# RWKV attention plus SMeLU MLP on one core: four batches across the partitions, attention in 32-row array tiles, orders from a list scheduler

## The chip, the cores and the metric

The kernel runs on one core of a Trainium2 chip. The metric is device microseconds of one execution. The two executions of before differ by 0.4% (196.12 and 197.0 us); an execution more than 1.5% above the fastest of its kernel is called slow here and is not compared. The profile is one execution, taken by the hardware profiler; its span differs from the median time, by 2.5 us in before.

## The reference

Four batches of 768 tokens go through a linear attention with 8 heads of 48 and a decay per channel; the result, 3072 tokens of 384, goes through an MLP with 2048 hidden units and a piecewise quadratic activation (SMeLU).

```python
# r, k, v: (4, 8, 768, 48); w, u: (8, 48)
for t in range(S):
    kt, vt, rt = k[:, :, t], v[:, :, t], r[:, :, t]
    cur = einsum('bhd,bhe->bhde', u[None] * kt, vt)
    y[:, :, t] = einsum('bhd,bhde->bhe', rt, state + cur)
    state = w[None, :, :, None] * state + einsum('bhd,bhe->bhde', kt, vt)

x = y.transpose(0, 2, 1, 3).reshape(3072, 384)
h = x @ w_in                                        # (3072, 2048)
g = where(h >= 1, h, where(h <= -1, 0, (h + 1) ** 2 / 4))
out = g @ w_out                                     # (3072, 384)
```

Both kernels work in chunks of 128 tokens: inside a chunk a masked matrix of scores, between chunks a state. Both compute `Square(0.5*h + 0.5)` for the activation, prove with norms that |h| stays under 1, and redo the MLP in general form if it does not.

## The kernel before

A *unit* is one batch's chunk of 128 tokens: 24 units, each with its tokens on the 128 partitions. Two units make one block of 256 tokens for the MLP, 12 blocks in all.

```python
def load():                          # one unit: 128 tokens on 128 partitions
    b, c = units[i]
    for name, src in (("K", k), ("R", r), ("V", v)):
        t = io.tile([128, H, D], F32, name=name, tag=name)       # 6 buffers each
        nc.sync.dma_start(out=t, in_=src[b, :, t0:t0 + C, :].rearrange("h s d -> s h d"))   # 192-byte rows

def s_at(i):                         # scores: two 64-row array tiles
    for p in range(NP):
        for s in range(2):
            mm(AT_p[s][:, p, :], KT[rows, p, :], RT[rows, p, :], start=True, stop=True)
    ...                              # mask on VectorE

def s_y(i):                          # output and state of one unit
    for p in range(NP): mm(pair(y, p), RT[:, p, :], Tbd[b][:, p, :], ...)        # history
    for h in range(H):  mm(y[:, h, :], AT[h % 2][:, h // 2, :], V[:, h, :], ...) # inside the chunk
    for p in range(NP): mm(st[:, p, :], pair(Kw, p), pair(V, p), ...)            # new state
    for h in range(H):               # the u term, on VectorE, head by head
        nc.vector.scalar_tensor_tensor(x[:, h*D:(h+1)*D], V[:, h, :], diag[:, h:h+1], y[:, h, :], ...)

def layer1(m, n):                    # 6 matmuls of 256 columns, then the activation
    for f in range(2):
        for kk in range(nKb):
            mm(h_p[:, f, :], w_in_sb[:, kk, ...], xT[m][:, :, kk, :], ...)
    g = gT[m][:, 2*n:2*n+2, :]
    nc.scalar.activation(g, h_p, AF.Square, bias=0.5, scale=0.5)     # contiguous read and write

# [cut] layer2: 4 matmuls of 384 columns; the order of work is written by hand
# and refined by the framework's own scheduler
```

## Time and profile before

| | before |
|---|---|
| time, median of 2 | 196.56 us (196.12 to 197.0) |
| profiled span | 199.1 us |
| first layer-1 matmul | 25.0 us |
| last MLP matmul | 193.6 us |
| MLP matmuls, back to back | 125.6 us (96 groups at 0.655, 96 at 0.65) |

The profile's first part gives, for each engine, busy microseconds, their share of the span, and instructions. PE is TensorE's matmuls, PEld its weight loads, DVE VectorE, ACT ScalarE, POOL GpSimd. The second part cuts the span into 40 slices: a digit is a busy share in tenths, PEclk the clock granted to TensorE in tenths, DMA the busy share of the 16 DMA engines, GB/s what they moved. Then come the DMA packets and the instruction-fetch queue, and the chain of waits: the work that ended last, followed back, shared out by engine. Of the page of before:

```profile
span 199.1 us, 4592 instructions
PE 172.3 (87%) x1686; PEld 125.7 (63%) x1686; DVE 111.8 (56%) x354; ACT 122.0 (61%) x251; POOL 110.8 (56%) x144
...
PE   0263598998989999999999959999999999999990
PEclk9999999999999999999999979999999999999999
DMA  4999989999969999999999998334315022020202
GB/s 96 201 258 264 250 195 221 243 181 268 262 131 244 173 193 169 258 195 173 253 162 216 165 168 206 76 74 132 64 35 153 2 66 66 9 79 0 82 3 89
DMA packets 100444, 30.25 MB, mean 152 GB/s; under 512 B 93504, under 2 KB 98880, under 8 KB 100416
...
q8 instruction: 15, 0.25, 0.6%
...
PE 66%; DMA 5%; DVE 4%; ACT 2%; POOL 1%; issue 1%; ACTq 0%; DVEq 0%
```

TensorE is the bound: it is nearly full from a quarter of the span on, and it is two thirds of the chain.

The groups of instructions: line, engine, operation, output<-input, shapes, count | busy us, mean ns of one | idle before, and what ended it. Two groups of before:

```profile
L285 ACT ACTIVATE gT<-h_p 128x512 bf16<-128x512 f32 x96 | 56.8, 598 | 44.9 <-PE h_p L279 42.6
L238 DVE SCALAR_TENSOR_TENSOR x<-V,diag,y 128x48 bf16<-128x48 bf16 x192 | 35.8, 257 | 18.5 <-PE y L227 11.1
```

The activation takes 598 ns, less than the 0.655 us of the layer-1 group that feeds it.

The timeline lists runs of instructions: start, length, what, and in brackets the idle time before and its cause. TensorE of before, a stretch in the steady part:

```profile
129.38 0.81 PE L279 MATMUL h_p<-xT_201,w_in_sb 128*128 128x256 bf16 x6
130.03 0.19 PE L227 MATMUL y<-V,AT_2273 128*128 128x48 bf16 x1
...
130.45 0.23 PE L206 MATMUL AT_p_2389<-RK 48*128 48x128 bf16 x1
...
130.78 0.83 PE L279 MATMUL h_p<-xT_202,w_in_sb 128*128 128x256 bf16 x6
```

Small attention matmuls of one unit lie between MLP groups; there is no idle time. One unit's scores take from 130.45 to 130.78, 0.33 us for 8 matmuls.

### The profile page before, as it was taken

How to read it: one execution, taken by the hardware profiler on the slowest of the kernel's cores; microseconds unless marked ns; L12 is line 12 of the kernel's file. 1: busy time of each engine (PE TensorE's matmuls, PEld its weight loads, DVE VectorE, ACT ScalarE, POOL GpSimd, SP SyncE). 2: the span in 40 equal slices, each digit the busy share in tenths (PEclk: the TensorE clock that was granted, in tenths of full speed). 3: DMA queues.
4: the chain of work that ended last, by engine and by line, in shares of the span. 5: the costliest groups of instructions: out<-in, count | busy, mean ns of one | idle time of the engine just before them, and what ended most of it. 6: DMA issues, size and time to landing. Idle time of an engine off the chain costs nothing.

```text
span 199.1 us, 4592 instructions
## 1 busy us (share of the span) xinstructions
PE 172.3 (87%) x1686; PEld 125.7 (63%) x1686; DVE 111.8 (56%) x354; ACT 122.0 (61%) x251; POOL 110.8 (56%) x144
## 2 busy tenths in 40 slices
PE   0263598998989999999999959999999999999990
PEld 0141476776867677866777547677667677777750
DVE  4179979994867608842867643776576464200110
ACT  3657769999887547936558326567555356454540
POOL 7496756989976999967679386857221000000000
PEclk9999999999999999999999979999999999999999
DMA  4999989999969999999999998334315022020202
GB/s 96 201 258 264 250 195 221 243 181 268 262 131 244 173 193 169 258 195 173 253 162 216 165 168 206 76 74 132 64 35 153 2 66 66 9 79 0 82 3 89
DMA packets 100444, 30.25 MB, mean 152 GB/s; under 512 B 93504, under 2 KB 98880, under 8 KB 100416
## 3 DMA queue, kind: packets, MB, share of 16 engines
q1 hardware_dynamic: 100416, 29.90, 75.1%
q8 instruction: 15, 0.25, 0.6%
q14 instruction: 13, 0.11, 0.2%
HBM read 20.84 MB, written 4.72 MB: 128 GB/s over the span
## 4 chain that ended last, share of the span: by engine, by line
PE 66%; DMA 5%; DVE 4%; ACT 2%; POOL 1%; issue 1%; ACTq 0%; DVEq 0%
PE o_p L297 28%; PE h_p L279 26%; DVE x L238 3%; DMA xT_201<-x 3%; DMA R<-in_r_dram 2%; PE y L227 2%; PE y L224 2%; PE st L235 1%; PE xp L265 1%; PE tr L194 1%; ACT gT L285 1%; ACT RK L197 1%; POOL RKW_173 L173 0%; POOL KU L177 0%; PE tr L196 0%
## 5 line engine op out<-in xcount | busy, mean ns | idle before, releaser
L285 ACT ACTIVATE gT<-h_p 128x512 bf16<-128x512 f32 x96 | 56.8, 598 | 44.9 <-PE h_p L279 42.6
L297 PE MATMUL o_p<-w_out_sb,gT 128*128 128x384 bf16 x384 | 73.5, 327 | 0.0
L279 PEld LDWEIGHTS <-w_in_sb 128*128 128x128 bf16 x576 | 54.5, 99 | 14.5 <-issue 3.4
L297 PEld LDWEIGHTS <-gT 128*128 128x128 bf16 x384 | 36.2, 98 | 19.3 <-issue 0.7
L238 DVE SCALAR_TENSOR_TENSOR x<-V,diag,y 128x48 bf16<-128x48 bf16 x192 | 35.8, 257 | 18.5 <-PE y L227 11.1
L176 POOL TENSOR_TENSOR KU<-K,u_bc 128x384 f32<-128x384 f32 x24 | 24.5, 1021 | 1.9 <-DVE diag L213 1.6
L177 POOL TENSOR_TENSOR KU<-KU,R 128x384 f32<-128x384 f32 x24 | 24.3, 1013 | 0.3
L301 DVE COPY o_sb<-o_p 128x384 f32<-128x384 f32 x12 | 6.7, 555 | 23.8 <-PE o_p L297 23.7
L197 ACT COPY RK<-tr 128x1024 bf16<-128x1024 bf16 x12 | 12.2, 1014 | 3.9 <-PE tr L196 3.8
L182 POOL CAST V<-V 128x384 bf16<-128x384 f32 x16 | 8.1, 503 | 11.3 <-DVE x L238 7.0
L206 PEld LDWEIGHTS <-RK 48*128 48x128 bf16 x192 | 8.3, 99 | 9.5 <-issue 4.2
L213 DVE TENSOR_REDUCE diag<-KU 128x8 f32<-128x384 f32 x24 | 13.1, 546 | 2.1 <-POOL KU L177 1.9
L265 PE MATMUL xp<-ident,x 128*128 128x128 bf16 x36 | 7.9, 236 | 5.6 <-DVE x L238 5.1
L301 ACT COPY o_sb<-o_p 128x384 f32<-128x384 f32 x12 | 5.7, 476 | 7.5 <-PE o_p L297 6.4
L173 POOL TENSOR_TENSOR RKW_171<-K,Winv 128x384 bf16<-128x384 f32 x6 | 6.0, 997 | 6.9 <-ACT Winv L137 3.5
L279 PE MATMUL h_p<-xT_201,w_in_sb 128*128 128x256 bf16 x48 | 7.4, 302 | 2.5 <-DMA xT_201<-x 2.5
L173 POOL TENSOR_TENSOR RKW_177<-K,Winv 128x384 bf16<-128x384 f32 x6 | 6.2, 1029 | 6.1 <-PE st L235 3.9
L265 PEld LDWEIGHTS <-x 128*128 128x128 bf16 x36 | 3.6, 101 | 8.9 <-DVE x L238 8.0
L194 PE MATMUL tr<-ident,RKW_171 128*128 128x128 bf16 x12 | 1.4, 249 | 8.8 <-POOL RKW_171 L173 8.8
L173 POOL TENSOR_TENSOR RKW_173<-K,Winv 128x384 bf16<-128x384 f32 x6 | 6.6, 1094 | 3.6 <-DMA K<-in_k_dram 1.8
L279 PE MATMUL h_p<-xT_195,w_in_sb 128*128 128x256 bf16 x48 | 7.7, 311 | 0.1
L173 POOL TENSOR_TENSOR RKW_175<-K,Winv 128x384 bf16<-128x384 f32 x6 | 6.4, 1072 | 2.1 <-DMA K<-in_k_dram 1.6
(356 smaller groups left out, 321.9 us busy)
## 6 DMA issues: line engine op xcount, KB each, us to landing
K<-in_k_dram SPq DMA_DIRECT2D x24, 192.0 KB, 4.9
R<-in_r_dram SPq DMA_DIRECT2D x24, 192.0 KB, 4.7
V<-in_v_dram SPq DMA_DIRECT2D x24, 192.0 KB, 4.9
out_dram<-o_sb SPq DMA_DIRECT2D x24, 192.0 KB, 2.3
w_in_f<-in_moe_w_in_dram SPq DMA_DIRECT2D x4, 768.0 KB, 5.7
w_out_f<-in_moe_w_out_dram SPq DMA_DIRECT2D x4, 768.0 KB, 5.9
w_bc<-in_w_dram SPq DMA_DIRECT2D x1, 192.0 KB, 3.5
u_bc<-in_u_dram SPq DMA_DIRECT2D x1, 192.0 KB, 4.3
```

Source lines behind the costliest of these rows:

```text
L173: nc.gpsimd.tensor_mul(Kw[:, :, 0:D], K, Winv)
L176: nc.gpsimd.tensor_mul(KU, K, u3)
L177: nc.gpsimd.tensor_mul(KU, KU, R)
L197: nc.scalar.copy(RK, tr)
L206: mm(AT_p[s][:, p, :], KT[rows, p, :], RT[rows, p, :], start=True, stop=True)
L213: nc.vector.reduce_sum(diag, KU, axis=mybir.AxisListType.X)
L238: nc.vector.scalar_tensor_tensor(x[:, h * D : (h + 1) * D], V[:, h, :], diag[:, h : h + 1], y[:, h, :], op0=ALU.mult, op1=ALU.add)
L265: nc.tensor.transpose(xp[:, kk, :], x[:, kk * 128 : (kk + 1) * 128], ident)
L279: mm(h_p[:, f, :], w_in_sb[:, kk, (2 * n + f) * 128 : (2 * n + f + 1) * 128], xT[m][:, :, kk, :], start=(kk == 0), stop=(kk == nKb - 1),)
L285: nc.scalar.activation(g, h_p, AF.Square, bias=0.5, scale=0.5)
L297: mm(o_ps[m][j], gT[m][:, f, j * C : (j + 1) * C], w_out_sb[:, f, :], start=(f == 0), stop=(f == nN - 1))
L301: (nc.scalar.copy if j else nc.vector.tensor_copy)(o_sb, o_ps[m][j])
```

## The change

The intent is to make attention cheap on TensorE and VectorE. All four batches share the partitions: batch b has partitions 32b to 32b+31, and each partition holds four neighbouring tokens ("four-token slots"), so a row of a load is 4 x 48 x 4 = 768 bytes. Products of one batch use only its 32 rows or columns of the array, so that four batches can go in separate array tiles. The u term becomes 16 matmuls with an identity. Because slots scatter tokens, the activation puts the tokens back in order by the pattern of its write. A list scheduler in the kernel, with a duration written down for each operation, orders all engines, and fills TensorE's early waits with dummy "warm-up" matmuls.

```diff
     def load(c, name, hh=None):
+        for b in range(B):                       # four transfers, 32 partitions each
+            nc.sync.dma_start(
+                out=t[name, c][qu[b], hs(hh)].rearrange("q h j d -> q h (j d)"),
+                in_=src[b, hs(hh), c*C:(c+1)*C, :].rearrange("h (p j) d -> p h (j d)", j=J),
+            )
 ...
+    def scores(c, jj, hh):                       # 32 matmuls a group, 4 groups a chunk
+        for p in range(2):
+            for j in range(2):
+                for s in range(2):
+                    for b in range(B):
+                        mm(A[qu[b], s, p, j], KT[rows[s], jj+j, 2*hh+p, qu[b]],
+                           RT[rows[s], :, 2*hh+p, qu[b]], start=True, stop=True)
 ...
+    def ymm(c, hh=None):
+        # 64 history matmuls, 128 inside the chunk, 16 for the u term, in one piece
 ...
+    def state_mm(c):
+        # 128 matmuls, in one piece
 ...
     def smelu(m, n):
-        nc.scalar.activation(g, h_p, AF.Square, bias=0.5, scale=0.5)
+        g = t["g", m][:, 2*n:2*n+2, :].rearrange("p f (u q i) -> p (f u) i q", u=UB, i=J)
+        h_p = t["h", m, n].rearrange("p f (u i q) -> p (f u) i q", u=UB, i=J)
+        nc.scalar.activation(g, h_p, AF.Square, bias=0.5, scale=0.5)
 ...
+    RING = dict(f=7, W=1, Vb=2, RK=1, AT=1, VD=1, x=2, g=3, o_sb=3, sq=2, a=2, h=2, o=2)   # buffers
 ...
+    def warm(count):                             # dummy matmuls, 221 in all
+        for i in range(count):
+            mm(w_p[:, 0:128], ident, ident, start=True, stop=True)
 ...
+    op(("sm", m, n), "ACT", 0.52, (smelu, m, n), [("L1", m, n)], 0)       # planned duration in us
+    op(("y", c, hh), "PE", (1.15 + 0.4 * (c > 0)) / n_y, (ymm, c, hh), needs, d + 10, ...)
+    op(("st", c), "PE", 0.55, (state_mm, c), ...)
 # [cut] one op(...) for every operation, and the scheduler's loop
```

Casts, norms and the MLP's matmuls are as before. Eight of 24 units are transposed on TensorE (before 12), the others by DMA.

## The prediction

> **What bounds the kernel now.** TensorE: 66% of the chain of waits, 54% in the two MLP layers. On the chain a layer-1 group (6 matmuls of 256 columns) takes 0.655 us and a layer-2 group (4 of 384) 0.65 us; 96 + 96 need 125.6 us. The first starts at 25.0 us (timeline), the last ends at 193.6, the span ends at 199.1 (unprofiled 196.6). So 168.6 us hold 125.6 of MLP and 43 us of attention matmuls, transposes and holes; 25 + 5.5 us are head and tail.
>
> In the first 36 us layer 1 trickles behind prep and casts. At 113.9 to 116.5 us TensorE waits for a DMA transpose (5.4 us on the chain) behind an input load (3.6 more). The 40 slices show the DMA engines at 80 to 100% until 117 us; 93,504 of 100,444 packets are under 512 B (192-byte rows).
>
> **What the change does.**
> 1. 768-byte loads: a quarter of the input packets. [...] this trace shows only that 192-byte loads ran at 200 to 260 GB/s with full engines. I expect over 280 GB/s in the head and no TensorE wait on a late load or transpose (-3 to -5 us), although DMA transposes now serve 16 of 24 units, not 12.
> 2. Attention in array tiles, four batches at once. [...] score matmuls at 28.26 us start in pairs, a pair each 55 ns. But a score group between MLP groups takes 0.33 us and not 0.22: about 0.1 us for a change of tile shape, both ways. Before, four units cost about 5.9 us of TensorE without transposes (scores 3.4, y and state 2.5). After, my estimate: scores 4 x 0.42 = 1.7; y 2.2 (tiny matmuls at 25 ns a round, 4 shape changes); state 0.8: 4.7 us. So about 1 us for each of six chunks, 6 us, not the tiles' factor of four. Fewer units transposed on TensorE (8, not 12): 2.5 us.
> 3. DVE loses 192 small multiply-adds (35.8 us busy, 257 ns each) for 12 double copies shared with ACT [...]; POOL gains a product. Off the chain in the steady part, it pays only in the head.
> 4. List-scheduled order and warm-up matmuls: MLP starts near 20 us, [...] without the trickle: with the holes of 40 to 60 us, -8 us.
>
> **Sum.** Start 20 + MLP 125.6 + attention of five chunks 23.5 + transposes and norms 3.5 + residual holes 4 = 176.6; tail 5 gives a span of 181, less the 2.5 us between span and time: 178; the order may do better than my holes, so 176.
>
> Predicted: 176 us, range 167 to 188. Chances: faster 0.93, same 0.04, slower 0.03.
>
> **What would show it.** First layer-1 matmul at 18 to 21 us; DMA packets near 35,000; PE busy above 90% from 20 us on; each scores group 0.3 to 0.45 us; no TensorE wait over 1.5 us after 40 us; MLP groups unchanged at 0.65 us; POOL busy near 115 us, DVE below 95.
>
> **What would make it wrong.** Small tiles not overlapping (128 weight loads a chunk in turn, at the 99 ns a record shows, would add 10 us a chunk and make it slower); single buffers for transposed inputs or scores making TensorE wait each chunk; DMA transposes of 128 x 2048 over 8 us; permuted ACT writes in the activation over 0.6 us; or, the other way, free tile changes: then 168.

The sum comes, as it says, to 176.6 us at the last MLP matmul, a span of 181, a time of 178 and then 176. But "over 280 GB/s" is the author's estimate and was not shown by before, where slices with the DMA engines at 9 tenths moved 162 to 268 GB/s. That four tiles run at once, as the attention term needs, was an estimate too: before shows two. Its trace has the other numbers of that step: output matmuls start 25 ns apart (28.02 to 28.14 us); the first score matmul starts 0.12 us after the last of them (28.26), and the next MLP group 0.15 us after the last score matmul (28.44 to 28.59), where score pairs follow each other at 0.06. "About 0.1 us for a change of tile shape" is an estimate from these starts. Of the 23 slices before 117 us two had the DMA engines under 80% (4 and 6 tenths).

## More of the kernel before

The fetch queue moved 15 packets for TensorE's 3,372 instructions.

"issue", time in which an engine waited for nothing that the profile shows, is 1%.

## The result, and the profile after

| | before | after |
|---|---|---|
| time, median of 2 | 196.56 us | 263.0 us (262.0 to 263.99) |
| ratio of after to before | | 1.338, 95% interval 1.313 to 1.363 |
| span of the profile | 199.1 us | 262.2 us |
| mean granted clock | 0.990 | 0.882 |
| first layer-1 matmul | 25.0 us | 47.7 us |
| ScalarE busy | 122.0 us | 177.0 us |

A ratio, here and below, is the mean time of one kernel's fast runs over that of the other's in the same rounds, so it is not quite the ratio of the medians quoted. The kernel is a third slower and its output is correct. The same lines of the page of after:

```profile
span 262.2 us, 8617 instructions
PE 201.8 (77%) x3927; PEld 147.7 (56%) x3927; DVE 112.0 (43%) x109; ACT 177.0 (67%) x210; POOL 101.3 (39%) x53
...
PE   7578342966843869992979986999878996999992
PEclk9957755697997777998699996899999999999999
DMA  6979998404279419999427935371032710310012
GB/s 148 200 216 366 200 207 287 130 2 120 55 152 207 78 62 205 196 211 201 80 56 165 232 75 65 64 156 45 23 65 55 168 63 2 63 60 32 31 60 71
DMA packets 50730, 31.94 MB, mean 122 GB/s; under 512 B 25344, under 2 KB 49152, under 8 KB 50688
...
q8 instruction: 32, 0.52, 0.9%
...
PE 53%; ACT 21%; issue 15%; DMA 4%; DVE 4%; SPq 1%; DVEq 0%; ACTq 0%
```

"issue" grew from 1% to 15% of the chain and ACT from 2% to 21%. TensorE has 7,854 instructions and the fetch queue 32 packets, twice as many. The granted clock falls to 0.5 to 0.7 in slices 3 to 8, where TensorE has holes. That costs MLP time too: at least 15 of the 192 MLP groups of this trace took 1.2 to 1.5 us, nearly all in stretches at half clock, and 3 groups did in before. No run priced this apart; with the cures below the mean clock rises again, to 0.961 and 0.982. The activation's group, after:

```profile
L376 ACT ACTIVATE gT<-h_p 128x512 bf16<-128x512 f32 x96 | 122.8, 1337 | 17.4 <-PE h_p L365 17.1
```

The same arithmetic on the same 128x512 elements takes 1337 ns, and now it is longer than the matmuls it follows. Three stretches of TensorE's timeline of after:

```profile
147.68 0.81 PE L388 MATMUL o_p<-w_out_sb,gT 128*128 128x384 bf16 x4
148.43 0.42 PE L248 MATMUL A<-RK 48*32 48x128 bf16 x32
148.77 0.83 PE L365 MATMUL h_p<-xT,w_in_sb 128*128 128x256 bf16 x6
...
118.09 1.20 PE L289 MATMUL y<-Vb,AT 32*128 32x48 bf16 x128
119.22 0.34 PE L295 MATMUL y<-VD,ident 32*32 32x384 bf16 x4
124.73 0.54 PE L295 MATMUL y<-VD,ident 32*32 32x384 bf16 x12 [5.17 <-issue]
...
188.61 0.37 PE L295 MATMUL y<-VD,ident 32*32 32x384 bf16 x14
191.07 0.34 PE L295 MATMUL y<-VD,ident 32*32 32x384 bf16 x2 [2.09 <-issue]
```

The first shows that the tiles do what was asked: 32 score matmuls take 0.34 us (148.43 to 148.77), as long as 8 did before; and 128 small output matmuls take 1.13 us (118.09 to 119.22), 9 ns each. The other two show holes of 5.2 and 2.1 us *inside* one group of 16 equal matmuls, with nothing waited for, and cut at 4 + 12 in one place, 14 + 2 in the other. TensorE's waits, summed by cause (us in total, times, longest), say how many there are:

```profile
PE y L295 <- issue: 16.2, 4, 6.6
PE st L339 <- issue: 9.7, 4, 5.9
PE h_p L365 <- ACT gT L376: 5.2, 8, 1.2
...
PE y L289 <- issue: 4.6, 2, 4.3
```

Counting TensorE's instructions in the trace (weight loads, matmuls and the few of its queue's own), and taking the 16,384-byte packets of the instruction-fetch queue beside them, shows a pattern. The first three columns are the hole's start, the time to the next instruction's start and the number of instructions begun by then; then that number over 256, and the fetch packet nearest before the restart:

```
hole at   us     begun   /256     packet
 28.57   6.84     961    3.754     32.59 to  33.98
 37.98   6.10    1217    4.754     41.68 to  42.80
 80.17   4.51    2241    8.754     81.85 to  83.17
 88.69   1.37    2497    9.754     87.36 to  88.72
119.23   5.50    3521   13.754    121.74 to 123.05
156.03   1.73    4801   18.754    155.42 to 156.49
159.73   2.03    5057   19.754    158.88 to 160.29
188.65   2.42    6081   23.754    188.40 to 189.80
193.75   1.04    6337   24.754    192.21 to 193.46
219.96   2.64    7361   28.754    219.72 to 221.14
```

Every one of these holes begins at the same remainder of 256 instructions, in most the packet is under way when the hole begins or starts in it, and TensorE restarts 1.3 to 1.7 us after it has ended. They sum to 34.2 us: 12.9 in the head, 21.2 after 60 us. The four of 4.5 to 6.8 us lie in slices with the DMA engines at 9 tenths, the six of 1.0 to 2.6 us in slices at 5 tenths or less.

### The profile page after: what moved, and what is told of

It is laid out like the page before. It is cut to its first block, busy times and chain, and to the rows that moved or that the text cites. A ratio compares the mean times of both kernels' runs of the same rounds, so it can differ in the third digit from the quotient of the medians.

```text
span 262.2 us, 8617 instructions
## 1 busy us (share of the span) xinstructions
PE 201.8 (77%) x3927; PEld 147.7 (56%) x3927; DVE 112.0 (43%) x109; ACT 177.0 (67%) x210; POOL 101.3 (39%) x53
## 2 busy tenths in 40 slices
DMA packets 50730, 31.94 MB, mean 122 GB/s; under 512 B 25344, under 2 KB 49152, under 8 KB 50688
## 4 chain that ended last, share of the span: by engine, by line
PE 53%; ACT 21%; issue 15%; DMA 4%; DVE 4%; SPq 1%; DVEq 0%; ACTq 0%
PE o_p L388 20%; PE h_p L365 17%; ACT gT L376 15%; DMA R<-in_r_dram 3%; PE w_p L141 3%; PE y L289 3%; PE A L248 3%; PE st L339 3%; DVE RKW L187 3%; PE y L281 2%; ACT x L330 1%; PE y L295 1%; ACT o_sb L396 1%; ACT RK L233 1%; PE xp L312 1%
## 5 line engine op out<-in xcount | busy, mean ns | idle before, releaser
L376 ACT ACTIVATE gT<-h_p 128x512 bf16<-128x512 f32 x96 | 122.8, 1337 | 17.4 <-PE h_p L365 17.1
L365 PE MATMUL h_p<-xT,w_in_sb 128*128 128x256 bf16 x576 | 83.2, 285 | 7.1 <-ACT gT L376 5.2
L365 PEld LDWEIGHTS <-w_in_sb 128*128 128x128 bf16 x576 | 57.8, 102 | 26.3 <-issue 10.9
L260 DVE TENSOR_TENSOR AT<-A,umask 128x1024 bf16<-128x1024 f32 x22 | 26.0, 1218 | 14.7 <-PE A L248 14.7
L198 POOL TENSOR_TENSOR K<-K,u_bc 128x1536 f32<-128x1536 f32 (+1 forms) x6 | 18.7, 3124 | 25.8 <-DVE RKW L187 25.8
L187 DVE TENSOR_TENSOR RKW<-R,Wpow 128x768 bf16<-128x768 f32 (+1 forms) x8 | 26.9, 3376 | 0.0
L215 POOL TENSOR_TENSOR VD<-V,dg 128x768 bf16<-128x768 f32 (+1 forms) x8 | 17.2, 2152 | 18.7 <-DVE dg L207 18.7
L141 PE MATMUL w_p<-ident 128*128 128x128 bf16 x221 | 20.6, 265 | 3.8 <-ACT gT L376 2.2
L141 PEld LDWEIGHTS <-ident 128*128 128x128 bf16 x221 | 18.4, 123 | 5.5 <-issue 3.8
L202 POOL TENSOR_TENSOR K<-K,R 128x1536 f32<-128x1536 f32 (+1 forms) x6 | 19.0, 3173 | 0.5
L357 DVE CAST Tbd<-T 64x768 bf16<-64x768 f32 x5 | 15.5, 3095 | 2.6 <-POOL T L354 2.5
```

Of the source, the lines that this page charges most:

```text
L141: mm(w_p[:, 0:128], ident, ident, start=True, stop=True)
L187: eng.tensor_mul(t["W", c][:, :, off + h.start : off + h.stop, 0:D], jhd(t[name, c])[:, :, h], tab[:, :, h])
L198: nc.gpsimd.tensor_mul(t["KU", c][:, hs(hh)], t["K", c][:, hs(hh)], ub4[:, hs(hh)])
L202: nc.gpsimd.tensor_mul(KU, KU, t["R", c][:, hs(hh)])
L215: eng.tensor_mul(t["VD", c].rearrange("q j h d -> q h j d")[:, h], t["V", c][:, h], dg)
L260: nc.vector.tensor_mul(scores_tile(c, jj, hh), t["A", c, jj, hh], umask2[jj // 2])
```

## The experiments

Three theories, none excluding another:

- **A, the write.** The permuted bf16 write of the activation doubles it (598 ns in before, 1337 in after).
- **B, instructions.** TensorE's instructions come in blocks of 256, one 16,384-byte packet each (the ten holes above lie at one remainder of 256; 32 packets came for 7,854 instructions), and TensorE waits when it has used up a block before the next has come. Tiny matmuls in tiles use up a block in 1.13 us (128 matmuls and 128 weight loads), the MLP in about 17 (20 instructions in 1.3 us), so the tiles would make it wait.
- **C, narrow loads.** A load of 32 partitions moves fewer bytes per microsecond than one of 128 (tested below: 12.7 bytes per ns and engine against 18.1 with 768-byte rows, no loss with 192-byte rows).

Rivals: the holes are the cost of the array tiles themselves (changes of shape, waits that the trace doesn't show); the order is bad because the scheduler's durations are wrong; the head has too many loads, or too few buffers. Each ratio is against before in the same rounds, whose median was 198.8, 198.3, 199.8, 200.4 and 197.9 us in the five sets of runs. (The 200.4 had two slow runs of three; the fast one was 197.09.)

### The activation's write alone, in before

Before, with the activation's pattern of after. The tokens come out permuted: the result is wrong (relative error 0.048).

```diff
-            nc.scalar.activation(g, h_p, AF.Square, bias=0.5, scale=0.5)
+            nc.scalar.activation(
+                g.rearrange("p f (u q i) -> p (f u) i q", u=UB, i=4),
+                h_p.rearrange("p f (u i q) -> p (f u) i q", u=UB, i=4),
+                AF.Square, bias=0.5, scale=0.5,
+            )
```

> The kernel before, with one thing of the change: the activation of layer 1 reads and writes in the permuted order (stride of four elements, 8 bytes, in the bf16 output). Rows come out permuted, wrong on purpose. Theory A: mean of the activation 598 to about 1330 ns, ScalarE busy about 192 us, and ScalarE becomes what a block waits for: time 205 to 225 us. Rival (the slow activations of the kernel after come from something else there, such as PSUM or SBUF contention): mean stays near 600 ns and time near 196 us.

Measured: 214.48 us, ratio 1.083 (1.070 to 1.097). The group and the chain of that run:

```profile
L285 ACT ACTIVATE gT<-h_p 128x512 bf16<-128x512 f32 x96 | 121.6, 1345 | 12.1 <-PE h_p L279 11.7
...
PE 40%; ACT 37%; DVE 7%; issue 5%; POOL 4%; DMA 2%; SPq 2%; DVEq 0%; ACTq 0%; POOLq 0%
```

So A is real by itself, and the rival of contention in after is out: the pattern alone makes 598 ns into 1345 and costs 16 us in a kernel with nothing else changed; ScalarE goes from 2% to 37% of the chain.

### The activation contiguous, in after: three attempts

First, contiguous read and write, with the order put right in the stores: four per 128 tokens, 32 partitions each.

```diff
-        g = t["g", m][:, 2*n:2*n+2, :].rearrange("p f (u q i) -> p (f u) i q", u=UB, i=J)
-        h_p = t["h", m, n].rearrange("p f (u i q) -> p (f u) i q", u=UB, i=J)
+        g = t["g", m][:, 2*n:2*n+2, :].rearrange("p f t -> p (f t)")
+        h_p = t["h", m, n].rearrange("p f t -> p (f t)")
 ...
-        nc.sync.dma_start(out=out[t0:t0+C, :], in_=t["o_sb", m, u])
+        o4 = out[t0:t0+C, :].rearrange("(q i) d -> i q d", i=J)
+        for i in range(J):
+            nc.sync.dma_start(out=o4[i], in_=t["o_sb", m, u][qu[i]])
```

> The kernel after, with the activation of layer 1 writing its result contiguously; the token order is put right in the output stores instead (four stores of 32 partitions for one of 128). Theory A (the strided write of the activation holds the steady part back): the 96 activations fall from 1337 ns to about 600 ns, ScalarE busy from 177 us to about 106 us, time to 220 to 235 us. Theory B (TensorE runs out of instructions in the bursts of small matmuls, and this alone makes the kernel slow): activations as fast, but the time stays above 250 us, because the holes of TensorE without a releaser (about 34 us in all) stay. If both hold: 220 to 235 us with the holes still about 30 us.

Measured: 258.76 us, ratio 1.306 (1.294 to 1.317). The activation fell to 596 ns and ScalarE to 115.5 us busy, but the chain gave it back:

```profile
PE 42%; issue 20%; DMA 16%; SPq 8%; POOL 7%; ACT 2%; DVE 2%; POOLq 0%; DVEq 0%
PE o_p L387 18%; PE h_p L365 14%; DMA RK<-RKW 7%; DMA K<-in_k_dram 6%; POOL K L198 3%; SPq L401 3%; DMA R<-in_r_dram 3%; SPq L174 3%; PE y L289 2%; PE st L339 2%; PE A L248 2%; POOL K L202 2%; PE y L281 2%; POOL T L354 1%; PE y L295 1%
```

Theory A's range of 220 to 235 us was missed, and the holes at block edges did not shrink (39.7 us, 34.2 in after). L401 is the new store. Stores, loads and DMA transposes are issued from one queue, and in this run that queue waited 34.8 us in 7 places (up to 13.4) at L401 for the block to store. That such a wait holds back the transposes behind it fits the chain (DMA RK, 7%; SPq L401, 3%) but was not tried apart. The run mixes two edits and can't price A.

Second, the order put right where layer 1 reads: the matmul's moving operand is read with 64 bytes between elements.

```diff
-                    ..., xT[m][:, :, kk, :],
+                    ..., xT[m][:, :, kk, :].rearrange("p u (i q) -> p u q i", i=J),
```

> The kernel after with a contiguous write in the activation, and the token order put right where layer 1 reads its moving operand (strided read, same matmuls), so that the stores stay as they were: the run with four stores per block had held transposes back in the store queue. Theory A alone: activations 600 ns; time 225 to 245 us, below the 258.8 of that run by what the stores cost. Theory that neither A nor the instruction holes alone is worth much, because each hides behind the other and behind the chain from one chunk to the next: 245 to 258 us, with the holes near 34 us. If the strided read slows TensorE, the layer-1 groups take longer than 0.66 us, and the run says nothing of A.

Measured: 464.12 us (fast runs 459.21 and 459.56). The activation was 597 ns, but:

```profile
L365 PE MATMUL h_p<-xT,w_in_sb 128*128 128x256 bf16 x576 | 263.6, 607 | 0.6 <-issue 0.6
```

A group of six takes 263.6/96 = 2.7 us in place of 0.655. A scattered moving operand costs four times here, and the low clock of this run (mean 0.636) is not the reason: these matmuls start 430 ns apart at full and at half clock alike. Two more kernels of the same rounds were built on this read, one with the theory's other cures, one with measured durations in the scheduler:

> All three together: contiguous write with the strided read in layer 1, y and state products in pieces with two buffers, no warm-ups. If the holes and the activation are the two limits of the steady part and hide each other: 195 to 215 us, holes after 60 us below 6 us, ScalarE busy about 110 us. If a third limit (the chain of one chunk through weighting, transposes, scores, masks, y and state, on single-copy queues) is worth as much: 220 to 245 us.

> As the run with all three, but the scheduler plans with durations measured on the chip for the kernel after (for instance 3.0 us and not 0.5 for the cast of the state on VectorE, 3.0 and not 1.8 for the weighting there, 3.0 and not 1.7 for the decay on GpSimd) and 0.9 us between pieces. If the order itself, planned with durations that are too short, costs much: 5 to 15 us below the run with all three. If not: within 3 us of it.

They took 428.92 and 430.12 us. The read spoiled them; they say nothing of their own questions, which were asked again below.

Third, only the order of the activation's loops is exchanged: the write is contiguous, and the f32 read from PSUM is the strided side.

```diff
-        g = ...rearrange("p f (u q i) -> p (f u) i q", u=UB, i=J)
-        h_p = ...rearrange("p f (u i q) -> p (f u) i q", u=UB, i=J)
+        g = ...rearrange("p f (u q i) -> p (f u) q i", u=UB, i=J)
+        h_p = ...rearrange("p f (u i q) -> p (f u) q i", u=UB, i=J)
```

> The kernel after with the two loops of the activation's access pattern exchanged: the same mapping, but the bf16 output is written in order and the f32 input in the accumulator bank is read with a stride of 32. Nothing else differs. Theory A (the strided write to on-chip memory costs, not the permutation as such): 600 to 750 ns and not 1337; time 235 to 255 us, the rest hidden by the instruction holes and the chain of a chunk. If a strided read costs as much as a strided write: about 1300 ns, 263 us.

Measured: 253.4 us, ratio 1.258 (1.246 to 1.270), correct. Of that profile (a slow run):

```profile
L376 ACT ACTIVATE gT<-h_p 128x512 bf16<-128x512 f32 x96 | 57.1, 596 | 59.2 <-PE h_p L365 58.7
```

The very same elements move, and the cost is gone: it lay wholly in the write. The kernel gains about 12 us (mean of fast runs 251.3 against 263.0, on another chip).

### Bursts of tiny matmuls, in before

Does the instruction supply stall a kernel without any of the change's tiles, tile orders or waits? Before, with bursts of independent 32x32 matmuls put between its MLP groups: 192 while the DMA engines are busy, then 64, 192 and 384 in the quiet part.

```diff
+    BURST = {30: 192, 66: 64, 74: 192, 84: 384}
+    def burst(count):
+        z = ps_a.tile([128, 4, 32], F32, name="z", tag="a")
+        for i in range(count):
+            r = c = i % 4
+            rr, cc = slice(32 * r, 32 * r + 32), slice(32 * c, 32 * c + 32)
+            mm(z[cc, r, :], ident[rr, rr], ident[rr, rr], start=True, stop=True)
 ...
+        if g in BURST:
+            burst(BURST[g])
```

> The kernel before with four bursts of extra small matmuls (32 x 32 array tiles, 32 columns, into a spare bank, used by nobody): 192 near 95 us while input loads fill the DMA engines, then 64, 192 and 384 in the quiet part after 140 us. Theory B (instructions come in blocks of 256[...]): in the burst of 64 no hole or one below 1 us; in the quiet burst of 192 a hole of 1.5 to 3.5 us; in the quiet one of 384 holes of 5 to 8 us in all; in the busy one of 192 3 to 7 us; and each hole falls where the count of TensorE's instructions passes a multiple of 256 (same remainder). Rival (tiles of the array do not really run together and the records only hide it, or a change of tile shape costs microseconds): the hole grows in proportion to the number of matmuls, 64 included, is the same for the busy and the quiet 192, and falls at the end of a burst.

Measured: 210.63 us (one run, state unknown), correct. No hole of 0.5 us or more in the burst of 64, as expected, and none in the two of 192, against the expectation; in the burst of 384 TensorE's timeline shows two, 3.7 us in all where 5 to 8 were expected:

```profile
174.20 1.35 PE L446 MATMUL z<-ident 32*32 32x32 bf16 x133
176.66 1.18 PE L446 MATMUL z<-ident 32*32 32x32 bf16 x128 [1.11 <-issue]
180.39 0.80 PE L446 MATMUL z<-ident 32*32 32x32 bf16 x77 [2.55 <-issue]
```

Between the two holes lie exactly 128 matmuls with their 128 weight loads, and the holes begin at instructions 4289 and 4545: 16.754 and 17.754 blocks, the remainder seen in after. This settles what the holes are tied to: these matmuls all have one shape and depend on nothing, so neither a change of tile shape nor a hidden wait made them. It also corrects the size: the bursts of 384 instructions (192 matmuls and their weight loads) passed and the one of 768 stalled twice, so about one block of 256 is there in advance (an estimate from these counts).

### Output and state in pieces, in after

The 208 output matmuls of a chunk go in 7 pieces and the 128 state matmuls in 4, with MLP work of at least 1.3 planned us between; the transposed inputs and weighted inputs get a second buffer each. The activation stays slow.

```diff
-    RING = dict(f=7, W=1, Vb=2, RK=1, ...)
+    RING = dict(f=7, W=2, Vb=2, RK=2, ...)
+    GAP = 1.3
 ...
+                for piece in range(7):
+                    key = ("y", c, hh) if piece == 6 else ("yp", c, piece)
+                    op(key, "PE", 0.35 if piece < 6 else 0.36, (ymm, c, hh, piece), needs, d + 10, take,
+                       gap=needs[-1] if piece else None)
+                    needs, take = [key], []
 # [cut] the same for the state, in 4 pieces
```

> The kernel after with the same matmuls, but the y products of a chunk from the second on cut into seven pieces and the state products into four, with 1.3 us between pieces for MLP groups; two buffers instead of one for the weighted and the transposed inputs, which the longer chain needs. Theory B: the holes without a releaser after 60 us, 21 us before, fall below 8 us; the head's two (13 us) stay. Time: 245 to 255 us if the strided write (theory A) still holds ScalarE at 177 us busy; below 235 us if A is not a limit. Rival to B (holes belong to the small matmuls themselves): the holes stay near 21 us.

Measured: 257.87 us, ratio 1.298 (1.282 to 1.313). Holes at block edges after 60 us fell from 21.2 us to 1.8 (one), as B says, but the time hardly moved and missed its range: ScalarE was still 174 us busy, and the waits for the activation grew to 12.0 us in 26 places (5.2 in 8 before the edit; the profiled run was slow by 1.9%). Removing one bound alone only exposed the other.

### No warm-up matmuls

```diff
-    WARM_END = 40.0
+    WARM_END = 0.0
```

Alone, in after:

> The kernel after without the warm-up matmuls (221 of them, 442 instructions of TensorE with their weight loads, nearly two blocks of 256, all before 50 us). Theory B for the head: the two holes of 6.8 and 6.1 us before 45 us shrink to one of at most 6 us, or fall at other instructions at the same remainder of 256; the first layer-1 matmul starts at 36 to 43 us instead of 47.9, and the time falls by 4 to 10 us [...]. Rival (the warm-ups are needed; the holes are loads that came late): holes stay where they are in time, and the time is the same or grows.

Measured: 250.61 us, ratio 1.258 (1.246 to 1.269). And with the exchanged loops of the activation:

> The same without the warm-up matmuls. If the head's hole and the steady part add up: 10 to 15 us below the run with the exchanged loops alone, 222 to 243 us.

Measured: 241.93 us, ratio 1.206 (1.195 to 1.218), beside 253.4 for the same kernel with warm-ups in the same rounds. The 221 warm-ups and their weight loads are 442 instructions, 1.7 blocks, nearly all before 50 us, where the DMA share is 0.82 to 0.90. Without them one hole of about 6 us is left before the first layer-1 matmul in place of two, and that matmul comes at 37.6 us, not 48.2 (in a slow profile). Of these 10.6 us the holes account for 7.5 (13.7 to 6.2); the rest fits the warm-ups' own time, since 3.4 us of them stood between the holes and that matmul. So the gain is not all instruction supply. The warm-ups did not keep the clock up either: in after it stood at 0.60 from 25 to 50 us, half of it holes.

### All three cures together

Exchanged loops, no warm-ups, and the pieces with the two second buffers:

> Exchanged loops, no warm-ups, and the y and state products in pieces with two buffers. Theory that activation and instruction holes hide each other in the steady part: 200 to 220 us, holes after 60 us below 6 us. If the chain of one chunk (weighting, transposes in the store queue, scores, masks, y, state) is a third limit: 220 to 240 us.

Measured: 231.68 us, ratio 1.160 (1.150 to 1.171), 10 us under the kernel without pieces in the same rounds. Now the gain of the pieces shows, since the activation no longer hides it (the second buffers are in the same edit and were not run apart). At block edges one long hole, 5.87 us at 28.5, and one of 1.4 remain. TensorE's longest waits are now:

```profile
PE tr L229 <- DVE RKW L189: 14.3, 4, 8.1
PE h_p L368 <- DMA xT<-x: 7.1, 2, 6.8
```

The second comes at 106.6 us, where a transpose queues behind input loads: the chain there holds a load of 9.1 us and then the transpose of 6.0. The first layer-1 matmul is still at 37.1 us.

### The scheduler's durations

The kernel of the last section, with planned durations in nine lines set to measured ones (the activation 0.52 to 0.6, DMA transposes 1.3 to 1.9, the state's cast on VectorE 0.5 to 3.0, and so on).

> As the run before it in this list, but the order is planned with the durations that the chip showed (3.0 us for the weighting and for the cast of the state on VectorE, 3.0 for the decay on GpSimd, 1.4 for the squares on ScalarE, and so on). If the order planned with too short durations costs much: 5 to 15 us less than that run; if not, within 3 us of it.

Measured: 243.91 us, ratio 1.212 (1.196 to 1.227): 12 us *slower* than with the original durations in the same rounds. Better durations alone do not help this scheduler; whether another order would was not tried.

### The shape of the loads, in before

768-byte rows over 128 partitions, other tokens than asked (wrong):

```diff
-            nc.sync.dma_start(out=t, in_=src[b, :, t0:t0+C, :].rearrange("h s d -> s h d"))
+            h2 = 2 * (c % 4)
+            nc.sync.dma_start(
+                out=t.rearrange("q (h j) d -> q h (j d)", h=2),
+                in_=src[b, h2:h2+2, 0:4*C, :].rearrange("h (p j) d -> p h (j d)", j=4),
+            )
```

> The kernel before, with each K, R, V load fetching the same 192 KB as 256 pieces of 768 bytes on all 128 partitions (four neighbouring tokens of two heads), so the wrong rows, wrong on purpose. If longer pieces make loads faster, as the prediction said: packets of 768 B in 40 ns or less, 19 bytes per ns and engine or more, the median load lands in under 4 us instead of 4.9, the wait at 114 us goes, and the time falls by 2 to 6 us. If not: about 61 ns as in the kernel after, and the time within 1% of before.

192-byte rows, each load split in four of 32 partitions (correct):

```diff
-            nc.sync.dma_start(out=t, in_=src[b, :, t0:t0+C, :].rearrange("h s d -> s h d"))
+            for z in range(0, C, 32):
+                nc.sync.dma_start(out=t[z:z+32], in_=src[b, :, t0+z:t0+z+32, :].rearrange("h s d -> s h d"))
```

> The kernel before, with each K, R, V load cut into four of 32 partitions (same 192-byte pieces, correct). If it is the 32 partitions of one load that make the 768-byte packets of the kernel after slow: packets of 192 B go from 19 ns to 25 ns or more, and the time grows by over 5 us. If not: 17 to 21 ns and a time within 3% of before (288 more issues of about 0.45 us on the queue may still delay some).

Measured: 201.61 us with 768 bytes (the fast run of before beside it: 197.09), 255.34 us with the split loads (one run, state unknown). What a packet took, from the traces' DMA records:

```
                             bytes   mean ns   bytes per ns and engine
before                        192      19        10.1
192 B, 32 partitions          192      18
768 B, 128 partitions         768      42        18.1
after (768 B, 32 partitions)  768      61        12.7
after's weights, 128 part.   1536      76        20.2
```

Long rows on 128 partitions do move faster, and the head then shows 328 to 369 GB/s in slices 3 to 9:

```profile
GB/s 88 270 369 357 355 361 328 347 345 191 146 94 102 99 78 171 143 80 145 212 141 139 221 165 108 136 23 154 55 38 188 18 75 51 20 79 0 82 3 89
```

But before gained no time from it, although TensorE's wait at 114 us was gone: both expectations for the time were missed against that one fast run, and the steady part was not bound by the speed of its loads (18.1 bytes per ns and engine against 10.1). The head even got worse: the first layer-1 matmul came at 33.4 us instead of 25.0. The queue now issued six weight transfers of 768 KB in the first 22 us, not three, and an input load of the first 30 us took some 7.7 us to land, not about 6. (That this is the reason was not tried.) By 60 us the run had caught up. The split loads cost some 55 us for another reason. The chain of that run:

```profile
SPq 27%; PE 26%; DMA 26%; DVE 8%; issue 6%; POOL 5%; ACT 1%; POOLq 0%; DVEq 0%; ACTq 0%
```

SPq is the queue that issues the transfers: with 288 input loads in place of 72 (216 more, not the 288 of the expectation; the shortest issues of before took 0.39 to 0.44 us) it became a bound of its own, 27% of the chain, while the packets were no slower (18 ns against 19). After issues only 84, and SPq is 1% of its chain, so this is not after's main cost; in these runs a narrow load is slow per packet only where the row is long (61 ns against 42 at 768 bytes, 18 against 19 at 192).

### The loads of the head, in the kernel with all three cures

Four kernels ask why that kernel's first three blocks come at 37.1, 47.3 and 76.5 us against 25.0, 36.3 and 48.6 before. The second chunk reuses the first's inputs, so its 12 transfers are gone (wrong):

```diff
+        if c == 1:
+            t[name, 1] = t[name, 0]
+            return
 # [cut] the buffers' lists of users
```

> The run with exchanged loops, no warm-ups and pieces (231.7 us), but the second chunk takes the first chunk's K, R, V from on-chip memory and loads nothing; wrong on purpose. If the amount to load before the third block holds it back: its first matmul comes at 66 us or earlier instead of 76.5, and the time falls by 8 us or more. If the in-order chain on VectorE and GpSimd does: 72 to 77 us, time within 4 us.

The second chunk's inputs before three quarters of the weights:

```diff
-    first = "w K00 u R00 K01 R01 V00 V01 wc i0 i1 i2 i3 K1 R1 V1 o0 o1 o2 o3".split()
+    first = "w K00 u R00 K01 R01 V00 V01 wc i0 K1 R1 V1 i1 i2 i3 o0 o1 o2 o3".split()
```

> The run with exchanged loops, no warm-ups and pieces (231.7 us), with the second chunk's loads issued ahead of three of the four quarters of the first layer's weights; correct. In-order chain: the weighting and the K products of the second chunk start before 33 us instead of 40, the third block at 66 to 71 us instead of 76.5, time 222 to 229 us. Amount to load: third block within 3 us of 76.5, since the same bytes are needed by then.

Nine load buffers, not seven (`f=7` to `f=9`):

> The run with exchanged loops, no warm-ups and pieces (231.7 us), with nine staging buffers instead of seven; correct. If loads wait for free buffers: time 220 to 228 us and the wait of TensorE at 107 us (6.9 us) gone or halved. If not: within 3 us of 231.7.

Each chunk's load as one transfer over 128 partitions with the same 768-byte rows (other tokens: wrong):

```diff
-        for b in range(B):
-            nc.sync.dma_start(
-                out=t[name, c][qu[b], hs(hh)].rearrange("q h j d -> q h (j d)"),
-                in_=src[b, hs(hh), c*C:(c+1)*C, :].rearrange("h (p j) d -> p h (j d)", j=J))
+        nc.sync.dma_start(
+            out=t[name, c][:, hs(hh)].rearrange("q h j d -> q h (j d)"),
+            in_=src[c % B, hs(hh), 0:B*C, :].rearrange("h (p j) d -> p h (j d)", j=J))
```

> The same run (seven buffers), with each K, R or V load of a chunk made as one transfer over all 128 partitions (same bytes, same 768-byte pieces, rows of one batch instead of four, so wrong on purpose). If the shape of the loads is the term: 768-byte packets at 36 to 45 ns instead of 61, first layer-1 matmul at 28 to 33 us instead of 37.1, no wait of TensorE on a transpose at 107 us, time 212 to 224 us. If the work of four batches at once before the first block is the term: first matmul at 34 us or later and time above 227 us.

| edit | time, us | third block at, us |
|---|---|---|
| all three cures | 231.68 | 76.5 |
| no second loads | 231.82 | 77.4 |
| second chunk first | 232.22 (its fast run) | 74.8 (profile slow) |
| nine buffers | 229.26 (its fast run) | 77.9 (profile slow) |
| wide loads | 218.51, ratio 1.106 (1.076 to 1.135) | 71.0 |

Neither fewer loads, nor an earlier second chunk, nor more buffers mattered. (The first of these is not clean: its shared inputs hold their buffers longer, and the second layer's weights came late. It shows one thing all the same: its first layer-1 matmul came at 31.6 us, not 37.1, and the long hole was gone, 0.39 us at the same instruction 705 where it had been 5.87, and yet the time was the same. The earlier first block bought nothing while the third still came at 77 us.) The width of a transfer did: 768-byte packets went from 62 to 41 ns, the time fell by 11 to 13 us, the first layer-1 matmul came at 33.7 us (just outside the expected 28 to 33). TensorE's waits of that run, two of the list:

```profile
PE tr L228 <- DVE RKW L188: 14.6, 4, 10.3
...
PE h_p L367 <- DMA xT<-x: 1.1, 2, 0.8
```

The transposes no longer queue: the longest wait for one went from 6.8 us (at 107 us) to 0.8. And the long hole in the head, at instruction 705, shrank from 5.87 to 1.77 us, with another of 1.5 one block earlier. So the hole at this block shrank in both runs whose head input came faster or was less, here and without second loads (there the block's packet started at 26.3 us, not 31.6); that the input in front of it delays a block fits this and was not tried apart. One rival is open: the edit also cuts the input transfers from 84 to 21, and SPq, 8% of the chain before it, is gone from the chain after. Packet speed and number of transfers were not told apart.

### VectorE and GpSimd side by side

A reading of traces, with no run of its own; first the kernel with all three cures. VectorE and GpSimd there, in the head:

```profile
39.16 1.82 DVE L189 TENSOR_TENSOR RKW<-K,Winv 128x768 bf16<-128x768 f32 x2
40.89 5.06 DVE L189 TENSOR_TENSOR RKW<-R,Wpow 128x768 bf16<-128x768 f32 x2
```

```profile
40.19 2.45 POOL L200 TENSOR_TENSOR K<-K,u_bc 128x768 f32<-128x768 f32 x1 [17.44 <-DVE RKW L189]
42.72 2.41 POOL L204 TENSOR_TENSOR K<-K,R 128x768 f32<-128x768 f32 x1
45.09 2.52 POOL L200 TENSOR_TENSOR K<-K,u_bc 128x768 f32<-128x768 f32 x1
```

Two products of one shape take 1.82 us while GpSimd mostly rests (it starts at 40.19), and 5.06 while it works, 2.8 times as long. The scheduler plans 0.9 us for each. The same product of R at 128x1536 took 4.94 us beside GpSimd here (at 60.98) and 1.75 with GpSimd at rest in the run without second loads (at 68.75). In after the state's cast, one form (64x768), takes 0.56 us at 46.93, with GpSimd at rest, and 3.6 to 3.8 the four later times, each beside GpSimd's products. Not every operation is slower: the masks of after that read PSUM take 1.21 to 1.23 us either way. Before shows a spread on smaller tiles (557 ns at the shortest, up to 1353), but there it was not on the chain. Why GpSimd's work slows these operations was not shown, and what it costs after was not run apart.

## Why the prediction was wrong

The sum failed in two places, the start and what it added to the MLP between the first and the last layer-1 or layer-2 matmul. It read: start 20, MLP 125.6, attention, transposes and "residual holes" 31, tail 5.

| | predicted | after |
|---|---|---|
| first layer-1 matmul | 20 | 47.7 |
| from there to the end of the last MLP matmul | 156.6 | 209.6 |
| tail of the span | 5 | 4.9 |

**Step 4, the start near 20 us and "residual holes 4", is the step that failed.** The sum had no term for the supply of instructions, as if TensorE took them as fast as it can run them. It does not: 34.2 us of holes lie at block edges, two in the head among the warm-ups that were meant to help (taking these out: 10 to 12 us, not all of it holes) and the rest in or just after output and state groups run in one piece (in pieces: 10 us, once the activation was fast). In before this cost was hidden (issue 1% of the chain); here it is not (15%). The warning was readable in advance: 3,372 instructions before, and the diff adds hundreds of tiny matmuls a chunk.

**The activation was seen and not costed.** The prediction listed "permuted ACT writes in the activation over 0.6 us" under what would make it wrong, and gave it no term in the sum; the diff's own planned 0.52 us was taken. Measured: 1337 ns, 66 us more of ScalarE; 16 us in before by itself, about 12 in after.

**Step 1, "over 280 GB/s in the head", failed** because it looked at bytes in a row only. On 128 partitions 768-byte rows did reach 328 to 369 GB/s. But the change cut each load into quarters of 32 partitions: 61 ns a packet, and 148 to 216 GB/s in five of the first seven slices. For 768-byte rows the loss is 12.7 bytes per ns and engine against 18.1, and wide loads gained 11 to 13 us of time; for 192-byte rows these runs show no loss (18 ns a packet against 19). "35,000 packets" missed too, with 50,730: 22,528 are packets of 256 bytes, 1,408 for each of the 16 units transposed by DMA (16,896 for 12 before).

**Step 2, the tiles, was right.** A score group takes 0.34 us (said 0.3 to 0.45), the output groups about 2.2 us without holes, the state 1.0 to 1.2 (said 0.8): near the 4.7 us a chunk that it forecast, against its 5.9 before. That gain exists, and it is what brings the instructions. MLP groups stayed at 0.65 to 0.66, but for those at half clock.

**Step 3 was half right.** The 35.8 us of small VectorE operations went, but VectorE stayed at 112.0 us busy (said below 95): its eight products with R took 26.9 us and five casts of the state 15.5 (such a cast 3.6 to 3.8 us beside GpSimd's products, 0.56 alone). GpSimd, said near 115, was 101.3.

Undone one after another (means of fast runs):

| | us | step |
|---|---|---|
| after | 263.0 | |
| activation writes contiguously | 251.3 | 11.7 |
| no warm-ups | 241.5 | 9.8 |
| output and state in pieces, second buffers | 231.8 | 9.7 |
| wide loads (wrong result) | 218.5 | 13.3 |
| before, in the last rounds | 197.6 | |

The rows come from three sets of runs on different chips, so a microsecond or two of each step is uncertain, and an order of undoing is a choice. **Open: the last 21 us.** The progress of the MLP dates them. The time at which a given amount of MLP work had begun:

```
us of MLP work     1     20     40     60    100    125
before           27.0   61.2   87.1  111.8  167.8  193.2
wide loads       35.6   66.8   97.9  126.1  183.9  210.9
```

Some 9 us are there at the first block. In the change's form four batches must be loaded and prepared before any block is ready, where before needs two units; no run tried this. TensorE's waits for weighted inputs (14.6 us in that run) say little for it: 10.3 of them are the wait at the very start, which is 8.8 in before. And a rival: before itself, with wide 768-byte loads, had its first block at 33.4 us, as late as here, and made it up by 60 us. So these 9 us need not be part of the 21. The rest builds up to the middle and was not divided among VectorE's slower operations beside GpSimd, the larger part of DMA transposes, MLP groups at half clock, and the single order. No kernel beat before; the fastest correct one took 229 to 232 us.

## What to carry to other kernels

Small array tiles trade array time for instructions: count instructions per microsecond before believing the gain, since here a stretch that used 256 instructions in 1.13 us starved after about one block, and dummy matmuls spend from the same budget (taking 442 instructions of them out gave 9.8 us, not all of it holes). Where a layout has to be permuted on the way, cost every place it could be done with a measured duration: here the strided bf16 write cost 2.2 times (1337 ns against 596) and the strided moving operand 4 times (2.7 us against 0.655), while the strided f32 read from PSUM was free (596 ns). In these runs a transfer's rate went with the length of a row (10.1 bytes per ns and engine at 192 bytes, 18.1 at 768) and, with 768-byte rows, with the number of partitions (12.7 on 32). And a step listed under "what would make it wrong" has to be put into the sum with a probability, not left out of it.
